# Decode attention, parallel with a feed-forward block: V loaded through the ACT queue, K and the weights through the SP queue

## The chip, the cores and the metric

The kernel runs on one core of one Trainium2 chip. The metric is the device time of one execution in microseconds (us).

## The reference, cut to what matters

```python
xn = layernorm(x)                                    # x: 4 x 1 x 512, bf16
q  = (xn @ wq).reshape(4, 1, 32, 128).transpose(...) # 32 heads of 128
p  = softmax(q . k_cache * 128 ** -0.5)              # k_cache: 4 x 32 x 8192 x 128, bf16
o  = p . v_cache                                     # v_cache: the same shape
out = x + o @ wo + (silu(xn @ w_gate) * (xn @ w_up)) @ w_down
```

One query position is decoded for four sequences. Each of 128 pairs of head and sequence has 2 MB of K and 2 MB of V, each read once: 537 MB of 551 MB in all. The arithmetic is small beside that.

## The kernel before

The loop has one step per pair, m = head * 4 + sequence. In step i the K tile of pair i is transposed on DVE and multiplied on PE (scores), and the V tile of pair i - 4 is multiplied with the finished probabilities on PE (PV). At the last step of a head (i % 4 == 3) come the maxima, an exp on ACT, and a copy of the previous head's output from PSUM, also on ACT. All loads share nine slots of 16 KB per partition. All are issued on SP:

```python
def load_k(m):
    h, b = divmod(m, B)
    t_ = slot()
    nc.sync.dma_start(out=t_[:], in_=A_k_cache[b, h, :, :].rearrange("(p t) d -> p (t d)", p=P))
    k_tiles[m] = t_

def load_v(m, parts=1):
    ...
    for i in range(parts):
        nc.sync.dma_start(out=t_[:, i * w:(i + 1) * w], in_=src[:, i * w:(i + 1) * w])
...
def load_wo(half):                       # rows of 512 bf16: 1 KB each
    nc.sync.dma_start(out=t_[:].rearrange("p (h e) -> p h e", h=n),
                      in_=A_wo[half * n * P:(half + 1) * n * P, :].rearrange("(h p) e -> p h e", p=P))
...
for i in range(M + LP + 1):              # M = 128, LP = 4
    if i + 2 < M:
        load_k(i + 2)
    if 0 <= i + 2 - LP < M:
        load_v(i + 2 - LP, parts=4 if i + 2 - LP == M - 1 else 1)
    ...                                  # FFN weights at i = 5, wo at i = 115 and 116
    if i < M:
        for g in range(NTG):
            t_piece(i, g)                # DVE: transpose a quarter of K
            s_piece(i, g)                # PE: scores
        if bs == B - 1:
            max_1(hs)
    mp = i - LP
    if 0 <= mp < M:
        for k in range(NK):
            pv_chunk(mp, k)              # PE: 16 chunks
            if k == NK // 2 and i < M and bs == B - 1:
                max_2(hs)                # PE, DVE, then the exp on ACT
        if bv == B - 1:
            fin_1(hv)                    # ACT: copy of o_sb
```

## Time and profile before

| | before |
|---|---|
| median time | 1310.62 us (1310.60 to 1310.66) |
| span of the profiled run | 1308.9 us |
| moved | 551.5 MB, 427 GB/s in the flat part |
| PE busy | 83% |
| DVE busy | 53% |
| ACT busy | 4% |
| DMA on the chain that ended last | 91% |

The prediction below shows the lines of the profile and what it reads from them.

### The profile page before, as it was taken

How to read it: one execution, taken by the hardware profiler on the slowest of the kernel's cores; microseconds unless marked ns; L12 is line 12 of the kernel's file. 1: busy time of each engine (PE TensorE's matmuls, PEld its weight loads, DVE VectorE, ACT ScalarE, POOL GpSimd, SP SyncE). 2: the span in 40 equal slices, each digit the busy share in tenths (PEclk: the TensorE clock that was granted, in tenths of full speed). 3: DMA queues.
4: the chain of work that ended last, by engine and by line, in shares of the span. 5: the costliest groups of instructions: out<-in, count | busy, mean ns of one | idle time of the engine just before them, and what ended most of it. 6: DMA issues, size and time to landing. Idle time of an engine off the chain costs nothing.

```text
span 1308.9 us, 11179 instructions
## 1 busy us (share of the span) xinstructions
PE 1089.7 (83%) x4610; PEld 423.3 (32%) x4676; DVE 693.8 (53%) x887; ACT 48.6 (4%) x102; POOL 5.6 (0%) x11
## 2 busy tenths in 40 slices
PE   5888888888888888888888888888988888886887
PEld 2243333333333333333333333333333333332333
DVE  7634554554554564554565555455555555544542
ACT  1000000000000000000000000000000000000000
POOL 1000000000000000000000000000000000000000
PEclk8889999999999999999999899999999999997999
DMA  9999999999999999999999999999999999999996
GB/s 393 429 425 428 426 427 428 427 427 426 427 429 426 426 428 426 427 428 425 429 426 428 426 427 427 427 426 427 428 428 426 425 429 426 427 394 412 425 428 288
DMA packets 42210, 551.49 MB, mean 421 GB/s; under 512 B 4264, under 2 KB 8368, under 8 KB 8880
## 3 DMA queue, kind: packets, MB, share of 16 engines
q1 hardware_dynamic: 42160, 550.79, 99.5%
q8 instruction: 36, 0.59, 0.2%
q14 instruction: 14, 0.11, 0.0%
HBM read 550.77 MB, written 0.00 MB: 421 GB/s over the span
## 4 chain that ended last, share of the span: by engine, by line
DMA 91%; PE 5%; DVE 3%; issue 0%; SPq 0%; ACT 0%; DVEq 0%; ACTq 0%
DMA slot<-in_A_k_cache_dram 86%; DMA slot<-in_B_w_up_dram 3%; DMA slot<-in_A_v_cache_dram 3%; DVE kt L252 2%; PE oacc L72 2%; PE sps L72 2%; PE xps L72 0%; SPq L93 0%; PE mps L274 0%; SPq L85 0%; DVE mx L268 0%; DVE res L384 0%; DVE zq L243 0%; PE mps L72 0%; ACT o_sb L309 0%
## 5 line engine op out<-in xcount | busy, mean ns | idle before, releaser
L252 DVE STREAM_TRANSPOSE kt<-slot 128x1024 uint32<-128x1024 uint32 x512 | 593.6, 1212 | 300.1 <-DMA slot<-in_A_k_cache_dram 295.4
L72 PE MATMUL sps<-kt,zq 128*128 128x512 bf16 x1982 | 566.9, 415 | 196.7 <-DVE kt L252 176.4
L72 PEld LDWEIGHTS <-zq 128*128 128x128 bf16 x2048 | 208.9, 103 | 544.4 <-issue 375.9
L298 DVE RECIPROCAL rcp<-mps 128x4 f32<-128x4 f32 x32 | 5.8, 182 | 162.5 <-PE mps L72 162.5
L268 DVE TENSOR_REDUCE mx<-sps 128x1 f32<-128x512 f32 x32 | 22.1, 691 | 40.5 <-PE sps L72 40.5
L277 DVE TENSOR_REDUCE nm<-mps 128x4 f32<-128x64 f32 x32 | 7.2, 224 | 50.2 <-PE mps L274 50.2
L72 PE MATMUL xps<-ident_f,o_sb 128*128 128x4 f32 x256 | 33.1, 253 | 0.7 <-ACT o_sb L309 0.7
L72 PEld LDWEIGHTS xps<-ident_f,o_sb 128*128 128x128 f32 x256 | 31.1, 192 | 1.2 <-ACT o_sb L309 1.2
L243 DVE COPY zq<-qt 32x16 bf16<-32x16 bf16 x128 | 23.5, 183 | 1.3
L318 DVE TENSOR_TENSOR otn<-xps,rcp 128x4 bf16<-128x4 f32 x32 | 5.2, 162 | 34.3 <-PE xps L72 34.3
L309 ACT COPY o_sb<-oacc 128x512 f32<-128x512 f32 x32 | 18.8, 586 | 20.8 <-PE oacc L72 20.7
L72 PE MATMUL oacc<-slot,pt__5656 128*4 128x512 bf16 x64 | 14.6, 379 | 0.1
L72 PE MATMUL oacc<-slot,pt__4008 128*4 128x512 bf16 x64 | 14.6, 379 | 0.1
L72 PE MATMUL oacc<-slot,pt__367 128*4 128x512 bf16 x64 | 14.6, 379 | 0.0
L72 PE MATMUL oacc<-slot,pt__918 128*4 128x512 bf16 x64 | 14.6, 379 | 0.0
L72 PE MATMUL oacc<-slot,pt__2154 128*4 128x512 bf16 x64 | 14.6, 379 | 0.0
L72 PE MATMUL oacc<-slot,pt__3802 128*4 128x512 bf16 x64 | 14.6, 379 | 0.0
L72 PE MATMUL oacc<-slot,pt__1330 128*4 128x512 bf16 x64 | 14.6, 379 | 0.0
L72 PE MATMUL oacc<-slot,pt__5862 128*4 128x512 bf16 x64 | 14.6, 379 | 0.0
L72 PE MATMUL oacc<-slot,pt__6719 128*4 128x512 bf16 x64 | 14.6, 379 | 0.0
L72 PE MATMUL oacc<-slot,pt__1536 128*4 128x512 bf16 x64 | 14.6, 379 | 0.0
L72 PE MATMUL oacc<-slot,pt__1742 128*4 128x512 bf16 x64 | 14.6, 379 | 0.0
(204 smaller groups left out, 636.5 us busy)
## 6 DMA issues: line engine op xcount, KB each, us to landing
slot<-in_A_k_cache_dram SPq DMA_DIRECT2D x128, 2048.0 KB, 39.0
slot<-in_A_v_cache_dram SPq DMA_DIRECT2D x127, 2048.0 KB, 39.2
slot<-in_A_wq_dram SPq DMA_DIRECT2D x2, 2048.0 KB, 9.6
slot<-in_A_wo_dram SPq DMA_DIRECT2D x2, 2048.0 KB, 29.8
slot<-in_A_v_cache_dram SPq DMA_DIRECT2D x4, 512.0 KB, 28.3
slot<-in_B_w_gate_dram SPq DMA_DIRECT2D x1, 1792.0 KB, 38.5
slot<-in_B_w_up_dram SPq DMA_DIRECT2D x1, 1792.0 KB
slot<-in_B_w_down_dram SPq DMA_DIRECT2D x1, 1792.0 KB, 33.2
```

The lines of the kernel that those rows point to most:

```text
L72: nc.tensor.matmul(out_ap, lhsT=lhsT, rhs=rhs, start=start, stop=True, skip_group_check=True, **kw)
L243: nc.vector.tensor_copy(out=zq[h % 2][a * QB:(a + 1) * QB, :, :, XO + a * QB].rearrange("p b (j r) -> p r j b", r=2), in_=qt[a * QB:(a + 1 ...
L252: nc.vector.transpose(out=kt[:].bitcast(dt.uint32).rearrange("p (j t r) -> p t j r", j=2, r=QB), in_=src.rearrange("p (t j r) -> p t j r", ...
L268: nc.vector.reduce_max(out=mx[:], in_=s_ps[h][:], axis=AX.X)
L277: nc.vector.tensor_reduce(out=nm[:], in_=mps[:, 0:P].rearrange("p (a x g r) -> p x a g r", a=NQ, x=B, r=2)[:, :, :, :, 0], axis=AX.XY, op= ...
L298: nc.vector.reciprocal(out=r_[:], in_=mps[:, P:P + B])
L309: nc.scalar.copy(out=o_sb[:], in_=o_acc[h % 2][:])
L318: nc.vector.tensor_tensor(out=otn[:, h, :], in0=xps[:], in1=rcp.pop(h)[:], op=ALU.mult)
```

## The change

The intent: two streams of loads on two queues, so that V's loads no longer stand behind K's in one line of issues.

```diff
@@ load_v
         for i in range(parts):
-            nc.sync.dma_start(out=t_[:, i * w:(i + 1) * w], in_=src[:, i * w:(i + 1) * w])
+            nc.scalar.dma_start(out=t_[:, i * w:(i + 1) * w], in_=src[:, i * w:(i + 1) * w])
```

In the built program the instructions on PE and DVE stand as before. ACT's line now holds the 131 V issues in between: four V loads, the exp of a head, the copy of o_sb, four V loads, and so on.

## The prediction

> **What bounds the kernel now.** I read the page's chain of waits first, then its slices and queues, then the waits of the DMA queue, then a timeline of the last head. The page, its chain, its DMA slices, its queues and its issues:
>
> ```profile
> span 1308.9 us, 11179 instructions
> ...
> DMA  9999999999999999999999999999999999999996
> GB/s 393 429 425 428 426 427 428 427 427 426 427 429 426 426 428 426 427 428 425 429 426 428 426 427 427 427 426 427 428 428 426 425 429 426 427 394 412 425 428 288
> ...
> q1 hardware_dynamic: 42160, 550.79, 99.5%
> ...
> DMA 91%; PE 5%; DVE 3%; issue 0%; SPq 0%; ACT 0%; DVEq 0%; ACTq 0%
> ...
> slot<-in_A_k_cache_dram SPq DMA_DIRECT2D x128, 2048.0 KB, 39.0
> slot<-in_A_v_cache_dram SPq DMA_DIRECT2D x127, 2048.0 KB, 39.2
> ```
>
> DMA is 91% of the chain. The one queue kept the 16 engines occupied for 99.5% of the span and moved a flat 427 GB/s in all slices but the first, the two with the small rows of wo (394, 412) and the last. 550.79 MB at 427 GB/s is 1290 us of a 1309 us span. One 2 MB transfer (2.097 MB) at that rate is 4.9 us; a K and a V, the need of one step (one batch of one head), 9.8 us. A load lands 39 us after its issue, so eight loads are always outstanding: 39.1 / 4.9 = 8.
>
> The waits of the DMA queue say why it is eight:
>
> ```profile
> SPq L93 <- DMA slot<-in_A_k_cache_dram: 446.6, 108, 5.7
> SPq L102 <- DMA slot<-in_A_v_cache_dram: 433.2, 107, 5.5
> ```
>
> SP spends 880 of 1309 us waiting for a load of the same kind to land: the built program hands eight completion semaphores round in program order, so each load waits for the one eight before it. SP is idle by plan; its own issue time (0.33 us a load in the timeline) costs nothing.
>
> The timeline of the end, and the busy times of the last stretches (the last two columns are DMA share and GB/s):
>
> ```profile
> 1277.43 4.62 DVE L252 STREAM_TRANSPOSE kt<-slot 128x1024 uint32<-128x1024 uint32 x4 [5.22 <-DMA slot<-in_A_k_cache_dram]
> ...
> 1286.20 0.69 ACT L284 ACTIVATE p__6895<-sps,nb 128x512 bf16<-128x512 f32 x1 [37.68 <-DVE nb L281]
> ...
> 1287.15 0.59 ACT L309 COPY o_sb<-oacc 128x512 f32<-128x512 f32 x1 [0.17 <-PE oacc L72]
> ```
> ```profile
> 1280.00:1290.00 10.00, 9.16 (x40) 3.26 (x39) 4.00 (x7) 1.37 (x3) 0.00 (x0) 1.00 1.00 423
> 1290.00:1300.00 10.00, 9.23 (x50) 4.12 (x50) 0.34 (x2) 0.00 (x0) 0.00 (x0) 1.00 0.84 345
> 1300.00:1302.00 2.00, 2.00 (x14) 0.82 (x11) 0.00 (x0) 0.00 (x0) 0.00 (x0) 1.00 0.11 43
> ```
>
> K of the last step (127) landed at 1277.4; its softmax exp ran at 1286.2 and the copy of the previous head's output ended at 1287.74, 10.3 us after the landing. The data ran on without a hole to about 1300, and some 8 us of PV, transposition and wo followed.
>
> **What the Trainium skill says.** "DMA: Bandwidth & Descriptors", section "Issuing engines are not separate DMA queues": loads from SP and ACT run on the same 16 DMA engines and interleave; a second issuer only saves the sequencer's issue time. The trace agrees as far as it can: that time is 0.33 us of every 4.9, already hidden. The same page, "Queues, rings and completion order": SP and ACT each have one ring on each of the 16 engines, and an engine takes turns between rings packet by packet. K and V rows are both 16 KB here, so I take it as half the rate each while both have work; the before trace has one data queue and cannot show it. "HBM Reference", "Specifications (TRN2)": a core streaming alone measures about 425 GB/s, bounded by its 16 DMA engines, not by the memory. The trace's 427 agrees, so two queues find no bandwidth that one left.
>
> **The change part by part.**
> 1. Bytes: none added or removed. 128 V tiles (268.4 MB) move to ACT's queue, 282.4 MB stay on SP's. The sum at 427 GB/s stays 1290 us. Effect 0.
> 2. Issue: 131 DMA issues leave SP (no gain, it idled) and join ACT. At 0.33 us that is 43 us more on an engine that is 48.6 us busy of 1309. None sits on the chain by itself. PE's and DVE's order are unchanged.
> 3. ACT's order. SP's list was loads only; ACT's is, per head: two V loads, two more, the exp of the head, the copy of the previous head's output, then the next loads. ACT works in order, so the two V loads behind exp and copy cannot start when their slot is free, but only when the last step of the head is finished. The first of them could otherwise have gone about one step earlier. Conversely, the loads ahead of an exp wait for a V landed, or a K transposed, at least a step before that exp is due, so they don't delay it.
> 4. Does the DMA run dry in the middle? When ACT is held up in step i (the last of a head), still outstanding can be K(i+1) to K(i+4) on SP's ring and V(i-3), V(i-2) on ACT's. If K is just in time, the four K are 4 x 4.9 = 19.6 us of work against the 10.3 us until ACT goes on. If instead V is late, then at the landing of V(i-4) two V are left, 9.8 us, against 3.62 us of PV and 0.59 of copy. Either way one ring feeds the engines. Effect 0. Compute cannot become the bound: PE needs about 4.1 + 3.6 us a step and DVE 4.6 (plus 2 to 3 a head), against 9.8.
> 5. The end. After K(127) there is no K left to cover the hold-up. V(126) and V(127) stand behind the last head's exp and the copy of head 30. In the kernel before, five V were queued when K(127) landed (24.5 us: 1277.4 + 24.5 = 1301.9; seen about 1300). After, let T be the landing of K(127). The ring of V holds at most V(125) and part of V(123), V(124). I expect V to run about one step ahead of its need, since the weights of the FFN and wo (9.7 MB) go only through SP's ring and let V gain on K until V's ring empties at each hold-up. Then at T only V(125) is left: 4.9 us. V(126) is issued at T + 10.3; with about 1.3 us to its first packet (estimate, from the first small load, issued at 0.74 us and used soon after 2 us) the engines idle 10.3 + 1.3 - 4.9 = 6.7 us. If V and K were level, V(124) and V(125) would be left, 9.8 us, and the hole would be 1.8 us.
> 6. Start: V(0) and V(1) go out as soon as ACT is through with the two casts of q (17.2 us), before K(2) to K(4) instead of after them. That slows the first K, but the engines are busy meanwhile, so only the order changes. Effect 0.
>
> Sum: 1310.6 + 0 + 6.7 = 1317.3; with some weight on the level case, 1316.
>
> **The rivals.**
> - A: two rings hide the gaps between transfers and the rate rises. For: the 394 and 412 slices, at most (33 + 15) / 427 x 32.7 = 3.7 us. Against: the flat 427 and a packet median of 614 ns for 16 KB back to back. It would make 1306 to 1310.
> - B: taking turns costs the engines something per packet, or the two streams disturb each other in memory. Nothing in the profile speaks for or against, as there was one ring. 1% of 614 ns would be 13 us: 1325 to 1330.
> - C: head-of-line blocking on ACT starves compute in every head, a dry hole of a few us x 32 heads: 1400 or so. Against: step 4; it needs both rings empty together, and the slack is 5 to 9 us.
> - D: wholly hidden, also at the end, if V lags K by two steps or more: 1310.6.
>
> **Range and chances.** The engines' work fixes 1290 us plus start and tail, so I see no way to gain 2% and need rival C or a strong B to lose 2% (over 1337). Between D (1310) and a mild B on top of the end's hole (1327): predicted 1316 us, 1309 to 1327 for 8 in 10; faster 0.01, same 0.95, slower 0.04.
>
> **What will show it.** Two data queues, about 282 and 268 MB, adding up to 550.8 MB; middle slices still at 426 to 428 GB/s (else A or B). K's landing time stays about 39 us (four outstanding at half rate); V's falls to 20 to 30 us, since fewer V are outstanding. ACT's waits at V loads and the exps' dates within a head stay regular. In the end: a dip in DMA share between the last exp and the first of V(126), about 7 us, with the issue of V(126) just after the copy of o_sb; from data's end to the span's end still about 8 us. Wrong would be: holes once a head (C), a middle rate other than 427, or no hole at the end (D).

## The result

The changed kernel takes 1313.62 us (median; 1312.91 to 1313.74) against 1310.61, a ratio of 1.0022 (95% interval 1.0005 to 1.0039). A ratio here is the mean time of one kernel's fast runs over that of the other's of the same rounds, so it is not quite the ratio of the medians. Within 2% it is "the same", but the 3.0 us are well outside the spread of the runs, and the study is about them.

The page after, its lines that answer to those of before:

```profile
span 1311.8 us, 11347 instructions
...
GB/s 392 428 425 428 427 427 426 427 427 426 427 427 427 428 425 429 425 430 424 428 425 428 426 427 427 427 427 427 426 428 425 429 425 428 426 420 389 424 429 250
...
q1 hardware_dynamic: 23296, 282.35, 51.0%
q10 hardware_dynamic: 18864, 268.44, 48.3%
...
DMA 87%; PE 7%; DVE 3%; issue 1%; SPq 1%; ACT 0%; ACTq 0%; DVEq 0%
...
slot<-in_A_k_cache_dram SPq DMA_DIRECT2D x128, 2048.0 KB, 36.1
slot<-in_A_v_cache_dram ACTq DMA_DIRECT2D x127, 2048.0 KB, 33.0
```

There are two data queues now, with the sizes foreseen, and the middle runs at the same 427 GB/s: turns between two rings cost no bandwidth, and bring none. The dip of the wo loads is as deep as before (420, 389, 424 here; 394, 412, 425 there). Only the last slice is clearly emptier (250 against 288 GB/s), so the time is lost near the end. V lands 33 us after its issue, not in 20 to 30.

The chain that ended last, from 1218 us on, before. Columns: start, duration, what.

```profile
1218.60 29.28 DMA slot<-in_A_k_cache_dram
...
1263.74 33.21 DMA slot<-in_A_v_cache_dram
1296.96 0.04 issue
1297.00 6.22 PE oacc L72 x32
1303.22 0.02 issue
1303.25 0.02 ACTq L309
1303.26 0.04 issue
1303.30 0.59 ACT o_sb L309
```

And after:

```profile
1220.14 22.43 DMA slot<-in_A_k_cache_dram
...
1243.86 3.46 DVE kt L252 x3
1247.32 0.02 issue
1247.34 34.44 DMA slot<-in_A_k_cache_dram
...
1289.68 0.27 PE mps L274
...
1290.68 0.79 ACT p__6895 L284 x2
...
1292.25 3.62 PE oacc L72 x16
...
1297.71 8.61 PE oacc L72 x48
1306.32 0.02 issue
1306.34 0.02 ACTq L309
1306.36 0.04 issue
1306.40 0.60 ACT o_sb L309
```

Before, the last thing that was waited for is a V tile; PE finishes it and the end follows. After, it is the last **K** tile: K(127) lands at 1281.8 instead of 1277.3, its exp runs at 1290.68 instead of 1286.20, and then PV of the four V tiles of the last head runs on PE with no wait for data, from 1292.25 to 1306.3, with only the short output chain of the head before between its two parts. K(127) is not slower on its way: it takes 34.4 us from issue to landing in both kernels. It is issued 4.5 us later, at 1247.34; in the kernel before it was

```profile
1242.85 0.33 SPq L93 DMA_DIRECT2D slot<-in_A_k_cache_dram  x1
```

In the chain above the issue follows the end of a transpose on DVE, that of K(123), at which a slot comes free; and K(123) is late itself, landed at 1242.56 against 1238.08 before. (Landings of single loads, here and below, are read from the traces load by load.)

The hole that the prediction put before V(126) does exist (a stretch of the windows view; last two columns DMA share and GB/s):

```profile
1289.00:1292.00 3.00, 2.54 (x12) 0.75 (x9) 1.05 (x4) 1.15 (x3) 0.00 (x0) 1.00 0.16 66
```

but in this chain nobody waits for what it delays. It is tempting all the same: the last V lands 3.2 us later than before (1305.2 against 1302.0), about as much as the time grew. That needed experiments.

### The profile page after: what moved, and what is told of

It is laid out like the page before. It is cut to its first block, busy times and chain, and to the rows that moved or that the text cites. A ratio compares the mean times of both kernels' runs of the same rounds, so it can differ in the third digit from the quotient of the medians.

```text
span 1311.8 us, 11347 instructions
## 1 busy us (share of the span) xinstructions
PE 1091.4 (83%) x4676; PEld 424.8 (32%) x4676; DVE 690.6 (53%) x887; ACT 48.7 (4%) x102; POOL 5.6 (0%) x11
## 4 chain that ended last, share of the span: by engine, by line
DMA 87%; PE 7%; DVE 3%; issue 1%; SPq 1%; ACT 0%; ACTq 0%; DVEq 0%
DMA slot<-in_A_v_cache_dram 75%; DMA slot<-in_A_k_cache_dram 12%; PE oacc L72 4%; DVE kt L252 3%; PE sps L72 2%; SPq L93 1%; PE xps L72 0%; PE mps L72 0%; PE mps L274 0%; DVE nm L277 0%; ACTq L102 0%; ACT p__6895 L284 0%; SPq L85 0%; PE yo_ps L72 0%; DVE pt__6909 L291 0%
## 5 line engine op out<-in xcount | busy, mean ns | idle before, releaser
L72 PE MATMUL sps<-kt,zq 128*128 128x512 bf16 x2048 | 550.2, 411 | 113.4 <-DVE kt L252 104.9
L72 PEld LDWEIGHTS <-zq 128*128 128x128 bf16 x2048 | 203.7, 102 | 447.2 <-issue 259.5
L72 PE MATMUL oacc<-slot,pt__4832 128*4 128x512 bf16 x64 | 16.1, 406 | 4.8 <-DMA slot<-in_A_v_cache_dram 4.8
L72 PE MATMUL oacc<-slot,pt__4008 128*4 128x512 bf16 x64 | 16.1, 407 | 4.3 <-DMA slot<-in_A_v_cache_dram 4.3
L72 PE MATMUL oacc<-slot,pt__2566 128*4 128x512 bf16 x64 | 16.1, 406 | 4.3 <-DMA slot<-in_A_v_cache_dram 4.3
L72 PE MATMUL oacc<-slot,pt__5862 128*4 128x512 bf16 x64 | 16.2, 407 | 3.9 <-DMA slot<-in_A_v_cache_dram 3.9
L72 PE MATMUL oacc<-slot,pt__5244 128*4 128x512 bf16 x64 | 16.1, 407 | 3.9 <-DMA slot<-in_A_v_cache_dram 3.9
L72 PE MATMUL oacc<-slot,pt__4420 128*4 128x512 bf16 x64 | 16.1, 406 | 3.9 <-DMA slot<-in_A_v_cache_dram 3.9
L72 PE MATMUL oacc<-slot,pt__2978 128*4 128x512 bf16 x64 | 16.1, 405 | 3.9 <-DMA slot<-in_A_v_cache_dram 3.9
L72 PE MATMUL oacc<-slot,pt__1536 128*4 128x512 bf16 x64 | 16.1, 405 | 3.6 <-DMA slot<-in_A_v_cache_dram 3.6
L72 PE MATMUL oacc<-slot,pt__3596 128*4 128x512 bf16 x64 | 16.1, 405 | 3.3 <-DMA slot<-in_A_v_cache_dram 3.3
L72 PE MATMUL oacc<-slot,pt__5656 128*4 128x512 bf16 x64 | 14.6, 379 | 5.0 <-DMA slot<-in_A_v_cache_dram 5.0
L72 PE MATMUL oacc<-slot,pt__3390 128*4 128x512 bf16 x64 | 14.6, 379 | 4.4 <-DMA slot<-in_A_v_cache_dram 4.4
## 6 DMA issues: line engine op xcount, KB each, us to landing
slot<-in_A_k_cache_dram SPq DMA_DIRECT2D x128, 2048.0 KB, 36.1
```

The lines of the kernel that those rows point to most:

```text
L72: nc.tensor.matmul(out_ap, lhsT=lhsT, rhs=rhs, start=start, stop=True, skip_group_check=True, **kw)
```

## The experiments

Twelve kernels ran, each with correct output, in five rounds each; of e4 the record holds four runs. The changed kernel itself was not run again beside them; the kernel before was. Times are medians; "before" beside them was 1310.52 to 1310.54.

| run | what it is | us | last K in use | exp of head 31 |
|---|---|---|---|---|
| before | one queue | 1310.6 | 1277.4 | 1286.2 |
| after | all V on ACT | 1313.6 | 1281.9 | 1290.7 |
| e1 | after, last two V on SP | 1314.7 | 1280.4 | 1289.3 |
| e2 | before, last two V on ACT | 1311.0 | 1277.6 | 1286.4 |
| e3 | after, last two V ahead of the exp | 1313.0 | 1280.6 | 1290.4 |
| e4 | after, 6.5 us of copies ahead of V(126) | 1321.3 | 1281.8 | 1290.6 |
| e5 | after, the same copies in heads 0 to 27 | 1313.3 | 1280.5 | 1289.9 |
| e6 | K on ACT, V on SP | 1315.8 | 1283.8 | 1292.6 |
| e8 | after, V(120) and later on SP | 1313.1 | 1277.8 | 1291.4 |
| e9 | one queue, V(123) ahead of K(127) | 1315.5 | 1282.3 | 1292.1 |
| e10 | after, V(108) and later on SP | 1310.6 | 1277.5 | 1286.2 |
| e11 | before, V(108) to V(119) on ACT | 1312.2 | 1277.6 | 1289.6 |
| e12 | before, V(120) and later on ACT | 1316.1 | 1283.0 | 1292.3 |
| e13 | before, shorter tail | 1310.2 | 1277.4 | 1286.4 |

The last two columns are the starts of the first transpose of K(127) and of the last exp in the profiled run, in us from the span's start. A profile shows one run: those of e8 (1314.13), e9 (1314.88) and e12 (1315.26) lie up to 1.0 us from the median of their kernel.

### First round: is it the hole at the end?

**e1_tail_sp.**

```diff
-            nc.scalar.dma_start(...)
+            (nc.sync if m >= M - 2 else nc.scalar).dma_start(...)
```

> The changed kernel, but the last two V loads, V(126) and V(127), go through the SP queue; 126 V loads stay on ACT. Theory 1 (the 3.0 us are one hole at the end, because V(126) and V(127) stand in ACT's order behind the last head's exp and the copy of head 30's output): the hole closes and the time is 1310.6 to 1311.0 us, as before. Theory 2 (two rings taking turns cost a little everywhere, 3 us spread over 256 loads): 126 of 128 V loads still take turns, so 1313.5. Theory 3 (ACT's order starves the DMA a little in every head, 3.0 us over 32 heads): 31 heads still have it, so 1313.5.

Measured: 1314.74 us (1314.61 to 1314.81; ratio 1.0032), slower than the changed kernel. The hole is gone and the last V piece lands at 1301.9, as early as before the change (1302.0), and yet the time is lost. All three theories miss. The profile shows what may make it even slower: V(126) on SP's ring now takes turns with V(124) and V(125) on ACT's, so those two, needed first, land later (1292.4 and 1298.6; 1287.3 and 1292.2 in the changed kernel), and PE waits for them, 2.30 and 0.74 us.

**e3_early_tail.**

```diff
-        if 0 <= i + 2 - LP < M:
-            load_v(i + 2 - LP, parts=4 if i + 2 - LP == M - 1 else 1)
+        if 0 <= i + 2 - LP < M - 2:
+            load_v(i + 2 - LP)
+        if i == M - 1:                       # ahead of the last exp
+            load_v(M - 2)
+            load_v(M - 1, parts=4)
```

> The changed kernel with all V loads on ACT, but V(126) and V(127) are written ahead of the last head's exp and copy in ACT's order. Theory 1: both are issued before the queue runs out, no hole, 1310.6 to 1311.0. Theories 2 and 3: all V loads still take turns and 31 heads are as they were, so 1313 to 1313.6.

Measured: 1312.99 us (1312.77 to 1315.06; ratio 1.0022). The same stretch of the windows view as above, now without a hole:

```profile
1289.00:1292.00 3.00, 2.28 (x11) 0.68 (x10) 1.25 (x4) 1.36 (x3) 0.00 (x0) 1.00 0.95 403
```

The engines are at 95% instead of 16%, the last V lands at 1302.1 instead of 1305.2, and the median is lower by 0.6 us of 3.0, within the spread of the runs. So the hole is not what sets the end. In this run the last head's exp still ran at 1290.41, and the last load on its chain is a K that comes into use at 1210.5, K(119):

```profile
1186.27 24.09 DMA slot<-in_A_k_cache_dram
```

For the last 101 us the chain runs over PE, DVE and ACT without a load.

**e2_only_tail_act.**

```diff
-            nc.sync.dma_start(...)                                     # in the kernel before
+            (nc.scalar if m >= M - 2 else nc.sync).dma_start(...)
```

> The kernel before, but V(126) and V(127) alone go through the ACT queue. They stand behind the same exp and copy. Theory 1 in full (the hold-up costs only when what is queued at that moment runs out first): in the kernel before, K has had the first turn, so V(124) and V(125) are still queued on SP when the copy starts at 1287.2 us, and V(125) lands at 1292.0; the hold-up ends some 3 to 4 us earlier than that, so no hole: 1310.6 to 1311.0. A simpler rival (a V load behind the last head's exp on ACT costs its delay, whatever is queued): 1313 to 1314. Theories 2 and 3: 1310.6, as only two loads are moved.

Measured: 1311.05 us (1310.74 to 1311.20; ratio 1.0003), at the upper edge of what the first theory said. Two V loads behind ACT's last exp cost about half a us, at the edge of the spread, where all loads before them stood in one queue. They do not cost 3.

**e4_delay_last.**

```diff
         osb[h] = o_sb
+        if h == H - 2:
+            for _ in range(10):
+                nc.scalar.copy(out=fill_b[:], in_=fill_a[:])   # 128x512 float32
```

> The changed kernel with ten idle copies (128x512 float32, SBUF to SBUF) on ACT after the copy of head 30's output, ahead of V(126), in the last head alone. By the copies of o_sb (0.59 us) they take 4 to 6 us together. Theory 1: the DMA is already dry when V(126) is issued, so each us of delay is a us of time: 1313.6 plus the copies' time, 1317.5 to 1319.5. Theories 2 and 3: 5 us in one of 32 heads, off the chain as they see it: 1313.6 to 1313.8.

Measured: 1321.29 us (1320.08 to 1323.96; ratio 1.0085), 7.7 us over the changed kernel, above the range. The copies took 6.47 us and V(126) was issued at 1297.9 instead of 1291.7. The timeline of this run has PE waiting for it:

```profile
1305.58 7.90 PE L72 MATMUL oacc<-slot,pt__6922 128*4 128x512 bf16 x32 [4.68 <-DMA slot<-in_A_v_cache_dram]
```

No such wait stands in the changed kernel. So a hold-up on ACT at the end can set the time, if it is long enough; without the copies it ended before PE needed V(126). The wait is 4.68 of the 7.7 us. The 32 multiplications after it took 7.90 us, where the changed kernel's 48 took 8.97 us, or 5.98 for 32: 1.9 us more. That may be PE's clock, which was granted at 0.50 from 1306 to 1308 us, just after the wait, and at 1.00 in the changed kernel; it was not tested.

### Second round: the last K

The theory now was that the end hangs on the landing of K(127) and on what PE has to do in series from there.

**e9_one_swap** (one queue, the kernel before).

```diff
-        if i + 2 < M:
+        if i + 2 < M - 1:
             load_k(i + 2)
         if 0 <= i + 2 - LP < M:
             load_v(...)
+        if i + 2 == M - 1:
+            load_k(i + 2)
```

> The kernel before, one queue, with one pair of loads exchanged: V(123) ahead of K(127). No load goes through ACT, no hole can come of a hold-up. New theory: K(127) lands one transfer (4.9 us) later, at 1282.2, the exp of head 31 at 1291.1, and with the 15.6 us from exp to the last copy of o_sb that the changed kernel and the one with early V loads had, the copy comes at 1306.7 against 1303.3 before: 1313.5 to 1314.5. The theory of the hole and that of two rings: 1310.6.

Measured: 1315.46 us (1314.88 to 1315.98; ratio 1.0038). One exchange of two loads in a single queue, with no second ring and no hole, costs 4.9 us, more than the change itself. K(127) is in use at 1282.3 as expected and the exp comes at 1292.1, 1 us later than expected, and the time is above the expected range. The direction and the mechanism are the new theory's, the size is not met: from the first transpose of K(127) to the transposition of the maxima passed 8.9 us here and 7.8 in the changed kernel. In that stretch PE had a lower clock, after a longer wait (6.74 us against 1.65). The windows view (the column before the last two is the granted clock of PE) of this run and of the changed kernel:

```profile
1284.00:1286.00 2.00, 1.78 (x5) 0.69 (x5) 2.00 (x3) 0.00 (x0) 0.00 (x0) 0.50 1.02 434
```
```profile
1284.00:1286.00 2.00, 1.87 (x9) 0.67 (x7) 2.00 (x3) 0.00 (x0) 0.00 (x0) 1.00 0.94 401
```

No run changed the clock alone.

**e8_last_fifo.**

```diff
-            nc.scalar.dma_start(...)
+            (nc.sync if m >= M - 8 else nc.scalar).dma_start(...)
```

> The changed kernel with V(120) to V(127) on SP, so that the last two heads have K and V in one queue in the old order, while 120 V loads stay on ACT. New theory: K(127) lands at about 1277.3 again, the exp of head 31 runs at 1286 and the time is 1310.6 to 1311.2. If the loss came from taking turns all along, or from ACT's hold-up in each head, 120 of 128 V loads still have it: 1313.4.

Measured: 1313.13 us (1311.62 to 1314.13; ratio 1.0018). K(127) landed at 1277.6, just as expected, and the time did not come back: the exp ran at 1291.4. The expectation failed, and so the landing of K(127) is not the whole cause. DVE still waited 1.50 us for K(127), but PE was behind: it had the work of earlier steps until 1284.6 and only then began the scores of K(127). The last load on the chain of this run is K(119):

```profile
1186.85 23.62 DMA slot<-in_A_k_cache_dram
```

K(127) was even issued later than in the changed kernel (1249.61), but landed 28.0 us after its issue instead of 34.4, with the V loads from V(123) on behind it in one queue. Here are the K tiles that DVE waited for in the stretch of the wo loads and after it, before the change (the bracket is the wait):

```profile
1182.37 4.62 DVE L252 STREAM_TRANSPOSE kt<-slot 128x1024 uint32<-128x1024 uint32 x4 [9.96 <-DMA slot<-in_A_k_cache_dram]
1198.17 4.62 DVE L252 STREAM_TRANSPOSE kt<-slot 128x1024 uint32<-128x1024 uint32 x4 [10.48 <-DMA slot<-in_A_k_cache_dram]
```

and in the changed kernel:

```profile
1197.18 4.62 DVE L252 STREAM_TRANSPOSE kt<-slot 128x1024 uint32<-128x1024 uint32 x4 [21.11 <-DMA slot<-in_A_k_cache_dram]
1210.46 4.62 DVE L252 STREAM_TRANSPOSE kt<-slot 128x1024 uint32<-128x1024 uint32 x4 [7.96 <-DMA slot<-in_A_k_cache_dram]
```

K(118) comes 14.8 us late and K(119) 12.3 us late. On SP's queue K(118) stands behind the first load of wo, and K(119) behind both. The queues of the changed kernel from 1165 to 1175 us (packets, MB, share of the engines' time):

```profile
q10 hardware_dynamic: 256, 3.87, 92.1%
q1 hardware_dynamic: 285, 0.32, 8.9%
```

Turns are taken packet by packet, 256 to 285. Read record by record, 217 of the 220 whole rows of V that the engines finish in this stretch are followed at once (within 5 ns) by a row of wo. But a row of V is 16 KB and a row of wo is 1 KB, so V got 3.87 MB and wo 0.32 MB. In that time SP's queue, with K(118) behind wo and K(119) not yet issued, hardly moves, while V moves at nearly the whole rate (387 GB/s).

**e5_delay_mid.**

```diff
         osb[h] = o_sb
+        if h < 28:
+            for _ in range(10):
+                nc.scalar.copy(out=fill_b[:], in_=fill_a[:])
```

> The changed kernel with the ten idle copies on ACT (6.47 us together in the run before) after the copy of o_sb in heads 0 to 27, and none in the last four. 28 times 6.5 us are 181 us of added hold-up. If the order on ACT starves the DMA in each head (the old theory 3, rival C of the prediction), the time grows by a large part of that, to 1400 us or more. If one of the rings always covers (step 4 of the prediction), nothing: 1313 to 1314.5. The new theory (below) also says 1313 to 1314.5.

Measured: 1313.32 us (1312.67 to 1316.99; ratio 1.0027). 28 hold-ups of 6.5 us, 181 us in all, cost nothing that shows beside runs that spread by 4.3 us: the order on ACT does not starve the DMA in the middle.

**e6_swap.**

```diff
-        nc.sync.dma_start(out=t_[:], in_=A_k_cache...)        # in the kernel before
+        nc.scalar.dma_start(out=t_[:], in_=A_k_cache...)
```

> K through ACT, V and the weights through SP. The first theory (a hole before V(126), which stands behind exp and copy) says no V is held up at the end, so 1310.6. The new theory: the end is set by when the last K lands, since from there run, one after the other, the scores of step 127, the exp and PV of four V tiles on PE; K(127) lands late when V takes turns with it. Here V still takes turns with K, and K(126), K(127) are issued behind the copy of head 31's predecessor: K(127) lands at 1281 us or later, against 1277.3 before, and the time is 1313.5 to 1318.

Measured: 1315.80 us (1314.36 to 1316.98; ratio 1.0040), as the new theory said. V is never behind ACT's work here, and yet it is slower than the changed kernel. The copy on ACT held up the issue of K(127) until 1254.6, and the last load on this run's chain is that K, from 1254.62 for 29.04 us.

### Third round: the two stretches, apart and together

These three undo or do the change by stretches: V(108) to V(119) cover the wo loads, V(120) to V(127) the last two heads.

**e10_wo_and_last_fifo.** `nc.sync` for m >= M - 20, else `nc.scalar`.

> The changed kernel with V(108) to V(127) on SP: 108 of 128 V loads stay on ACT, but both the stretch in which wo is loaded and the last two heads have one queue in the old order. Theory now: the 3 us have two causes, each enough for most of it: (a) K(127) lands late because V takes turns with it; (b) the two wo loads, whose packets are 1 KB, take turns one to one with V's packets of 16 KB, K(118) and K(119) behind them land 15 and 12 us late, and PE, which is then the bound, has not made that up when the last head ends. The run with the last two heads alone in the old order had K(127) at 1277.6 and still lost 2.6 us. With both removed: K(118) at 1182, exp of head 31 at 1286.2, 1310.6 to 1311.2. If turns cost something everywhere: 1313.

Measured: 1310.56 us (1310.39 to 1310.75) beside 1310.52; ratio 1.0001. With 108 of 128 V tiles still on ACT the whole loss is gone, and the last load on the chain is V(126) again, as before the change:

```profile
1263.80 33.18 DMA slot<-in_A_v_cache_dram
```

**e11_only_wo_turns.** `nc.scalar` for 108 <= m < 120, else `nc.sync`.

> The kernel before with only V(108) to V(119) on ACT: turns are taken in the stretch of wo and nowhere else. Cause (b) alone: K(118) lands at about 1197 instead of 1182.3, K(127) at 1277 to 1278, the chain at the end runs over PE without a wait for K, and the time is 1312.5 to 1313.5, as in the run with the last two heads in the old order. If (b) is not a cause: 1310.6.

Measured: 1312.24 us (1312.14 to 1312.79; ratio 1.0014): 1.7 us from twelve loads, just under the expected range. K(118) and K(119) are late as in the changed kernel, and from K(119) to the end the chain has no load in it:

```profile
1187.00 23.65 DMA slot<-in_A_k_cache_dram
...
1210.78 1.26 DVE kt L252
...
1289.55 0.79 ACT p__6895 L284 x2
```

K(119) comes into use at 1210.78 and the span ends at 1310.5, so the work from there, with no load on its chain, is 99.7 us. In the kernel before K(119) is in use at 1198.17 and the end is at 1308.9: 110.7 us. The slack is thus 11.0 us, and K(119) is 12.6 us late. That the difference is the 1.6 us by which the span grew is no test: it follows from how the four times are subtracted. A test are three other runs whose last load on the chain is K(119): from its use to the end pass 99.8 us in e5, 100.9 in e3 and 101.7 in e8. So the slack is 9 to 11 us, and the delay of 12 to 13 us exceeds it in all four. The spread goes with PE's granted clock (from 1210 to 1220 us 0.83 in e11, e5 and e3, 0.66 in e8; from 1270 to 1280 us 1.00, 1.00, 0.93 and 0.89), which no run changed alone.

**e12_only_last_turns.** `nc.scalar` for m >= M - 8, else `nc.sync`.

> The kernel before with only V(120) to V(127) on ACT: the stretch of wo is in the old order, the last two heads take turns. Cause (a) alone: K(118) at 1182.3, K(127) some us later than 1277.3 (up to 4.5), the exp of head 31 later by as much, and 1311.5 to 1314. If (a) is not a cause of its own: 1310.6.

Measured: 1316.11 us (1314.93 to 1317.13; ratio 1.0041): 5.6 us, above the expected range. V(120) and V(121), first on an empty ring, take turns with SP's long queue and overtake K(123) and K(124). K(124) is issued when it was before, and takes 39.1 us instead of 29.3 (1218.60 in the chain of before):

```profile
1218.62 39.13 DMA slot<-in_A_k_cache_dram
```
```profile
1248.01 4.62 DVE L252 STREAM_TRANSPOSE kt<-slot 128x1024 uint32<-128x1024 uint32 x4 [14.32 <-DMA slot<-in_A_k_cache_dram]
1257.77 1.25 DVE L252 STREAM_TRANSPOSE kt<-slot 128x1024 uint32<-128x1024 uint32 x1 [0.46 <-DMA slot<-in_A_k_cache_dram]
```

K(124) is in use at 1257.77 against 1247.90 before, 9.9 us late, and from there the chain again has no load in it. The same sum: 55.5 us from there to the end of this span (1313.3), 61.0 before, slack 5.5 us, exceeded by 4.4 us, again by subtraction alone. (The profiled run, at 1315.26, is faster than the median.)

The two parts, 1.7 and 5.6 us, do not add up to 3.0, and need not: both shift the same K tiles, and e12's queues, filled in the old order up to V(119), are in another state than those of the changed kernel. There K(124), the first K of the last head, lands at 1252.4 and not at 1257.7, and what delays the later K is in part the stretch before: the chain of the changed kernel goes from K(119) over PE to the issue of K(123), and over the transposes of K(123) to the issue of K(127). How the 3.0 us divide between the two stretches is left open; no run took the turns out of the wo stretch alone.

**e13_short_tail**, a try at beating both (one queue).

```diff
-            load_v(i + 2 - LP, parts=4 if i + 2 - LP == M - 1 else 1)
+            load_v(i + 2 - LP, parts=8 if i + 2 - LP == M - 1 else 1)
...
-                if k == NK // 2 and i < M and bs == B - 1:
+                if k == (NK // 4 if hs == H - 1 else NK // 2) and i < M and bs == B - 1:
```

> A try at beating both: the kernel before, one queue, with V(127) loaded in eight parts instead of four and the step from the maxima to the exp of the last head moved from the ninth to the fifth chunk of PV(123). In the kernel before the last landing (1302.0) and PE's own work from the exp on (1287.8 + 14.1 = 1301.9) end together, so both have to be shortened: exp 0.8 us earlier, last piece half as large. 1309.8 to 1310.4; 1310.6 if the last landing alone decides.

Measured: 1310.24 us (1310.13 to 1310.32; ratio 0.9998, interval 0.9984 to 1.0012). Its runs lie 0.3 us below those of before without overlap, but by the interval it is the same. The exp did not come earlier (1286.4), so that half of the edit did nothing. At 427 GB/s the 551 MB take 1290 us, so that only start and tail, some 20 us, are left to shorten; this try found nothing there.

## Why the prediction was right or wrong

The time was right: 1316 with 1309 to 1327, and it is 1313.6, on the side foreseen. The mechanism behind the number was wrong, and the time came out right by another route.

- **Step 1 and rivals A and B** (bytes and rate): right. Two rings, 282 and 268 MB, 427 GB/s. e10, at 1310.56 with 108 V tiles on ACT, shows that turns as such cost nothing measurable (interval 0.9988 to 1.0013).
- **Steps 2 to 4 as to ACT and the DMA, rival C** (issues on ACT are free, hold-ups in the middle are covered by the other ring): right, as e5 shows for the hold-ups.
- **Step 4, "Compute cannot become the bound"**: this is the step that failed. It compared the mean work of a step with the 9.8 us of its data. In the last ten steps that is the wrong comparison: few steps are left in which a delay could be made up, so the question is how long the serial work from a given K to the end is. e11 and e12 measure it: 99.7 us from K(119) and 55.5 us from K(124). The slack is only 9 to 11 and 5.5 us, and it shrinks to the 1.6 us of K(127) (31.5 us from its use to the end of the span before, 29.9 after, and 30.2 in e6 and 30.8 in e9, whose last load is that K too). In the changed kernel K(119) was 12.3 and K(127) 4.5 us late.
- **Step 5, the hole of 6.7 us**: the hole is there (the issue of V(126) at 1291.66, just after the copy of o_sb had started at 1291.63, nearly as foreseen), but it was sized wrongly and put on the path wrongly: the last V landed 3.2 us later than before, not 6.7. "I expect V to run about one step ahead of its need" did not hold: V is often late rather than early in the middle, as PE's waits show (us in total, times, longest), where the kernel before has next to none:

```profile
PE oacc L72 <- DMA slot<-in_A_v_cache_dram: 81.1, 54, 3.4
```

  So at the landing of K(127) two V tiles were left (they landed at 1287.3 and 1292.2), the level case of the prediction. (That case gave a hole of 1.8 us.) And the tail was taken as fixed behind the last byte ("some 8 us"; from the landing of the last V, at 1302.0 and not "about 1300", it is 6.9 us before the change), which was only true while the exp of the last head came early enough: in the changed kernel PE's own work from the exp on ends at 1306.3, after the last V landed (1305.2). Filling the hole bought at most 0.6 us (e3). But it was not far from the path: lengthened by 6.2 us it made PE wait 4.68 us (e4).
- **Step 6, "only the order changes. Effect 0"**: true of the start. But the order of landings was the very thing that cost time at the other end, and no rival named it. The prediction even used the turns packet by packet, and noted that wo has small rows, without putting the two together: one turn for 1 KB against one for 16 KB, with K behind it.
- **The signs**: K's time to landing was said to stay about 39 us and is 36.1; V's was to be 20 to 30 us and is 33.0, which fits with V not being ahead.

So the predicted 1316 was near by luck: 6.7 us for a hole that turned out not to set the end, and 3.0 us from a cause that was not in the sum.

What is shown: the loss lies in the stretch of the wo loads and in the last two heads (e10 removes all of it), K tiles land late there, and compute in series carries the delay to the end (the chains of e11, e12 and e9). What is not shown: why V lags in the middle rather than leads, how the 3.0 us divide between the two stretches, and whether PE's granted clock has a part in them (in the changed kernel it is 0.50 from 1190 to 1200 us, as PE waits 16.9 us for K(118), against 0.80 before; from 1210 to 1260 us it is 1.00 in both).

## What to carry to other kernels

This kernel, at the DMA's limit, gained nothing from a second queue (427 GB/s before and after). But the second queue replaced the written order by turns, and near the end the order counts: what the longest chain of work hangs on has to land first. Ask of each of the last loads how much serial work follows it, not only whether the engines are busy on average. A stream of small rows shared badly with one of large rows, 0.32 MB to 3.87, since the turns went row by row and not by bytes; what stood behind the small rows waited.

## What the Trainium skill lacked or had wrong

- "DMA: Bandwidth & Descriptors", "Issuing engines are not separate DMA queues": right that nothing is gained (427 GB/s before and after). It lacks that something can be lost by the changed order: 3.0 us for the whole change and 5.6 us for eight loads (e12).
- "DMA: Bandwidth & Descriptors", "Queues, rings and completion order": turns packet by packet agree with the trace (256 packets to 285 in 10 us). It lacks what follows for unequal rows: 3.87 MB against 0.32 MB, and a K tile behind the small rows 14.8 us late.
- The same section speaks of packets of some 9 to 17 descriptors. The trace's packet records here are single rows, 16 KB of V and 1 KB of wo, and the turns were by those: 217 of 220 rows of V were followed by a row of wo.
- No page says how much a queue of SP or ACT takes before the issuing engine itself stands. The K issue right behind the first load of wo took 29.47 us on SP before the change and 38.60 us after it, that behind the second 14.90 and 10.59 us; most other issues took 0.33 us.
